# A new rule for how many expert slots each pair of steps gets, and casts moved from VectorE to ScalarE

## The chip, the cores and the metric

The kernel runs on one core of a Trainium2 chip. The core has a matrix engine (TensorE, PE in the profile; its weight loads are the rows PEld), a vector engine (VectorE, DVE), an activation engine (ScalarE, ACT), a general engine that here issues indirect transfers (GpSimd, POOL), a queue engine for plain transfers (SyncE, SP), and 16 DMA engines that all queues share. The metric is the device time of one execution in microseconds (us); lower is better.

## The reference

The input is 2048 tokens of 512 numbers. They are normalised once (layer norm), and two branches are added to the input:

- **Attention** with 32 heads of 16 and one shared key and value head: `softmax(q k^T / 4) v`, then a projection with `wo`.
- **Experts.** For each token, 32 heads of two queries of 128 are scored against 64 keys each (`s1`, `s2`). The kernel contracts the query projection with the keys, so that a score costs one product with a combined weight. The best two of `s1` and of `s2` give four candidate sums; the best two of these name two of the 4096 experts and, by a softmax, two gates. An expert has a vector u and a vector v: the output adds `gate * gelu(x . u) * v` over 32 heads x 2 experts.

```python
top_e = jnp.take_along_axis(eidx, ord2, axis=-1)
g = _softmax(top_s, axis=-1)
ue = u[top_e]
ve = v[top_e]
act = _gelu(jnp.einsum("nd,nhkd->nhk", xf, ue))
out = jnp.einsum("nhk,nhk,nhkd->nd", g, act, ve)
```

## The kernel before

**Staging.** The 2048 tokens are four groups of 512 (phases 0 to 3). A prologue, whose order a scheduler decides, normalises and transposes all tokens, makes q, k, v and the weights and scores of the first eighth of the heads. All the rest is one loop over d, of 256 pairs of attention steps and 24 turns more (from line 1104), in an order written out by hand: each engine gets its instructions in the order in which the Python emits them. Below, a turn of this loop is called a step, and the first is 0.

**Attention in a step.** `att_steps` issues four pieces of scores on PE (L317), whose exps run on ACT (L320, four per step), and the products with the values (L331). After every eight steps ACT copies the sums out of PSUM into tile `e` (L339). Two of these copies make a block that is divided by its sums: a tile `rsb` is loaded, and DVE multiplies (`on`, L380). `e` and `rsb` take turns on one buffer.

**Experts, phases 0 and 1: gathered.** A *slot* is one candidate for a tile of 128 tokens: an indirect DMA of POOL's queue fetches 128 rows of u and v (`g`, 512 KB, L842), DVE forms the dot products with x (L854), and adds gate times v to the sum later (L889). Four slots share a chain of small DVE instructions (L863 to L865), a tanh on ACT (L870) and the weight `w` (L877). There are 512 slots. A ring of 12 buffers holds gathered rows; a slot's buffer comes free with its add, and only then can the gather 12 slots further on be issued. `lent` takes two buffers of the ring for the weights `wo` during parts of the loop. In each step `mid` runs the dots, then the adds that are ready, then up to four gathers.

**Experts, phases 2 and 3: dense.** Here all 4096 experts are multiplied with 512 tokens. A one-hot stage builds the table of gates: DVE makes one-hot tiles (L713 to L716), PE multiplies them (L729), ACT copies the result, and it goes through memory (`dg`). Then 32 blocks of 128 experts follow: PE multiplies x with u (`pact`, L781), DVE and ACT form the gated gelu (L800 to L808), PE multiplies with v (`pout`, L764), DVE adds to the sum (L767). ACT rounds the weights of a block and DVE makes the rest (L677, L678).

**Scores.** `item` (L531) makes the scores of 128 tokens and four heads: 12 matmuls, then 8 maxima and 8 index searches on DVE (L541, L543); after four items `batch` works out the indices and gates. In the first pass over the heads (phase 0), `wp_make` first builds the combined weights of four heads: PE multiplies (L486), ACT copies, PE transposes (`pwt`, L493), and DVE rounds the result to the matmul's format (L495) and subtracts that from the exact value (L496), so that `wk` holds a high and a low part.

**What sets the order.** `score_thread` is a Python generator with a planned cost for each piece of PE's expert work; `fill` draws pieces from it in each step until a plan that rises evenly over the loop is met. How many slots a step gets is counted by `pos`: up to step 191 it rises by fixed amounts that depend on whether the step has scores, one-hot work or blocks (`dense_on` 0, 2 or 1), and from step 192 on by an even share of what is left. Both PE's pieces and the slots' own order stay the same whatever `pos` does; `pos` decides beside which of PE's pieces a slot's dot and add stand in DVE's queue. The one-hot stages are steps 64 to 87 and 182 to 201; the blocks follow them, to steps 134 and 252.

PSUM has three buffers under the tag "x", which the score, transposition, weight, one-hot and block products take in turn.

Of the kernel before, what the change touches and what calls it, by code (L numbers as in the profile page):

```python
# [31 lines left out]
KC = D // P  # L32
NC = 8
TPH = GT
NPH = NGRP
NSP = 2
NB = 32
# [10 lines left out]
C_CUB = 0.044715 * C_IN  # L48
MOST = 4.8
UNIT = 0.235  # L50


@with_exitstack
def tile_kernel(ctx, tc, x, wq, wkv, wo, wqT, kT, uv, ub, vb, out):
    nc = tc.nc
# [409 lines left out]
    def wp_load(c, h):  # L465
        if late[0] is None or (c == 1 and h < 2):
            w = gtile(F32, (P, 2, D), "wqt") if c == 0 and h > 1 else big.tile([P, 2, D], F32, name="wqt", tag="wqt", bufs=2)
        else:
            w = late[0].tile([P, 2, D], F32, name="wqt", tag="gy", bufs=3)
        nc.sync.dma_start(w, wqT[4 * c + h].rearrange("(s p) d -> p s d", p=P))  # L470
        WC["raw", c, h] = w

    def wk_tile():
        return big.tile([P, 2, 512], F32R, name="wk", tag="wk", bufs=NWK)

    def wp_make(c):

        wt = [big.tile([P, 2, 512], F32, name="wt", tag="da", bufs=2) for _ in range(2)]
        for h in range(4):
            for n in range(4 * c + h + 1, min(4 * c + h + 3, 4 * NC) if late[0] else 4):  # L480
                if ("raw", n // 4, n % 4) not in WC:
                    wp_load(n // 4, n % 4)
            w = WC.pop(("raw", c, h))
            p = xtile("pw")
            for s in range(2):
                nc.tensor.matmul(p[s * E:(s + 1) * E, :], kTs[:, s, :], w[:, s, :], start=True, stop=True)  # L486
            nc.scalar.copy(wt[h // 2][:, h % 2, :], p)
            yield 0.9
        WC[c] = []
        for k in range(KC):  # L490
            p = xtile("pwt")
            for h in range(4):
                nc.tensor.transpose(p[:, h * P:(h + 1) * P], wt[h // 2][:, h % 2, k * P:(k + 1) * P], ident)  # L493
            wk = wk_tile()
            nc.vector.tensor_copy(wk[:, 0, :], p)  # L495
            nc.vector.tensor_tensor(out=wk[:, 1, :], in0=p, in1=wk[:, 0, :], op=OP.subtract)  # L496
            WC[c].append(wk)
            store(lambda k=k, wk=wk: nc.sync.dma_start(d_w[c][:, k], raw(wk[:])))
            yield 0.45

    def wp_read(n, ks=range(KC)):
        for k in ks:
            wk = wk_tile()
            nc.sync.dma_start(raw(wk[:]), d_w[SEQ[n][1]][:, k])
            WC.setdefault(n, []).append(wk)
# [6 lines left out]
    def item(n_, ti):  # L512
        ph, c = SEQ[n_]
        nph, nc_ = SEQ[n_ + 1] if n_ + 1 < len(SEQ) else (None, None)
        t = TPH * ph + ti
        g, j = divmod(t, GT)
        b, jb = divmod(ti, BT)
        if jb == 0:
            m8 = small.tile([P, BT, 8, 8], F32, name="m8", bufs=1)
            i8 = small.tile([P, BT, 8, 8], U32, name="i8", bufs=1)  # L520
            M8[ph, c, b], I8[ph, c, b] = m8, i8
        m8, i8 = M8[ph, c, b], I8[ph, c, b]
        p = xtile("psc")

        last = ti == TPH - 1
        more = nc_ is not None and not (ph >= NSP and c == NC - 1)
        read = more and n_ + 1 >= NC
        n = 0
        for k in range(KC):
            for a, bb in TERMS:  # L530
                nc.tensor.matmul(p, XT[g][k][:, a, j * P:(j + 1) * P], WC[n_][k][:, bb, :],  # L531
                                 start=n == 0, stop=n == 11)
                n += 1
            if read and ti == 0 and k < 2:
                wp_read(n_ + 1, range(2 * k, 2 * k + 2))
            if last and more and nph != ph:
                load_phase2_xt(nph, k)
            if k < KC - 1:
                yield 3 * UNIT
        for s in range(8):  # L540
            nc.vector.max(m8[:, jb, s, :], p[:, s * E:(s + 1) * E])  # L541
        for s in range(8):
            nc.vector.max_index(i8[:, jb, s, :], m8[:, jb, s, :], p[:, s * E:(s + 1) * E])  # L543
        if jb == BT - 1:
            batch(ph, c, b)
        yield 3 * UNIT

    IDX, G = {}, {}
# [95 lines left out]
    def dense(DG, after):  # L644
# [15 lines left out]
        def fetch_gates(b):  # L660
            if b < NB:
                if formed[0] < b - 2:
                    flush()
                gy = late[0].tile([P, 2, 512], F32, name="gy", tag="gy", bufs=3)
                nc.sync.dma_start(gy[:, 0, :], d_g[b])
                gates[b] = gy
# [31 lines left out]
        for n, src in enumerate((df1, df2, dgt)):  # L698
            if n == 2:
                yield None  # L700
            p = xtile("ptd")
# [7 lines left out]
        def onehot(q):  # L709
            if q < NQ:  # L710
                tb = q * TB
                oa = kt(F16, (P, P, TB))
                nc.vector.tensor_tensor(out=oa, in0=io, in1=bc(0, tb, P), op=OP.is_equal)  # L713
                ob = kt(F16, (P, NB, TB))
                nc.vector.tensor_tensor(out=ob, in0=io[:, :NB, :], in1=bc(1, tb, NB), op=OP.is_equal)
                nc.vector.tensor_mul(ob, ob, bc(2, tb, NB))  # L716
                OH[q] = oa, ob

        onehot(0)
        onehot(1)  # L720
        for q in range(NQ):
# [5 lines left out]
            p = xtile("pg")  # L727
# [26 lines left out]
        def sums():  # L754
# [4 lines left out]
            for j in range(GT):  # L759
# [7 lines left out]
                nc.vector.tensor_add(acc, acc, p)  # L767
                yield 6 * UNIT

# [3 lines left out]
        for b in range(NB):  # L773
            if b not in splits:
                flush()
            us, vs = splits.pop(b)
            p = xtile("pact")
            n = 0
            for k in range(KC):
                for a, c in TERMS:  # L780
                    nc.tensor.matmul(p, us[:, a, k * P:(k + 1) * P], XT[DG][k][:, c, :],  # L781
                                     start=n == 0, stop=n == 11)
                    n += 1
                if k == 0:
                    store(lambda b=b: fetch_gates(b + 1))
                    if b % 2 == 0:
                        later_split(b + 2)
                if k == KC - 1 and b == NB - 1 and after is not None:
                    wp_read(after, range(2))
                if b == NB - 1 and after is not None:  # L790
                    load_phase2_xt(SEQ[after][0], k)
                if k < KC - 1:
                    yield 3 * UNIT
            wd = late[0].tile([P, 2, 512], F32R, name="wd", tag="wd", bufs=4)
            if b not in gates:
                run(STORES)
            gy = gates.pop(b)
            g, y = gy[:, 0, :], gy[:, 1, :]

            nc.scalar.activation(y, p, AF.Square, scale=C_CUB ** 0.5)  # L800
            stt(y, y, C_IN, p, op0=OP.add, op1=OP.mult)
            stt(g, g, 1.0 / GS, p, op0=OP.mult, op1=OP.mult)
            LAST.append(lambda y=y: nc.scalar.activation(y, y, AF.Tanh))
            behind(lambda y=y, g=g, wd=wd: stt(wd[:, 0, :], y, 1.0, g, op0=OP.add, op1=OP.mult))
            behind(lambda y=y, g=g: stt(y, y, 1.0, g, op0=OP.add, op1=OP.mult))

            def rest(y=y, wd=wd):
                nc.vector.tensor_tensor(out=wd[:, 1, :], in0=y, in1=wd[:, 0, :], op=OP.subtract)  # L808
                formed[0] += 1

            behind(rest)
            held.append((wd, vs))
            yield 3 * UNIT
            if b % 2:
                later_split(b + 2)
                if ready:
                    yield from sums()
                else:
                    yield None
                ready, held = held, []  # L820
# [10 lines left out]
    NSL = len(slots)  # L831
# [62 lines left out]
    g_next, d_next, a_next, a_ready = [0], [0], [0], [0]  # L894
# [41 lines left out]
    def flush():  # L936
        posts()
        run(LAST)
        run(LATER)
        run(ON_ACT)  # L940
        run(BEHIND)
# [8 lines left out]
    def load_phase2_xt(g, k):  # L950
        if k == 0:
            XT[g] = []
        xt = big.tile([P, 2, 512], F32R, name="xt", tag="xt", bufs=4)
        nc.sync.dma_start(raw(xt[:]), d_xt[g - 1][k])
        XT[g].append(xt)
# [11 lines left out]
                yield from dense(ph, n + 1 if n + 1 < len(SEQ) else None)  # L967
                dense_on[0] = 0

    dense_on = [0]  # L970
    sgen = score_thread()
    spent = [0.0]

# [126 lines left out]
    with tc.manual_schedule(engines={E_.PE, E_.Activation, E_.DVE, E_.Pool, E_.SP}):  # L1100
        done0 = spent[0]
        half = STEPS // 2
        pos = 0.0
        for d in range(half + 24):


            if d < half * 3 // 4:
                pos += 2.4 if len(IDX) < NC * TPH else (1.9, 2.3, 1.5)[dense_on[0]]
            else:
                pos += max(0.0, NSL - pos) / max(half - 4 - d, 1)  # L1110

            todo = min(int(pos + 0.001), NSL) - d_next[0]

            def mid():
                post = POST[:]
# [97 lines left out]
```

## Time and profile before

| | us |
|---|---|
| median of three runs | 2036.56 |
| range of these runs | 2034.71 to 2038.64 |
| the profiled execution | 2035.25 |
| its span, first to last instruction | 2033.5 |

The profile has one execution. It gives each engine's busy time, groups of instructions with the idle time ahead of them and what ended it ("<-" names the releaser), and the timeline. L12 is line 12 of the kernel, and tile names stand as out<-in. Busy times of matmuls are modelled, and an instruction's time overlaps its neighbours' a little, so that for short instructions the spacing in the timeline is the better price. The mean granted clock of TensorE was 0.959. The loop's first exp starts at 148.6 us, the last ends at 2012.1.

### The profile page before, as it was taken

What the parts mean: (1) busy time and instruction counts of PE and PEld (TensorE: products, weight loads), DVE (VectorE), ACT (ScalarE), POOL (GpSimd) and SP (SyncE); (2) the same over time, 40 slices, a digit from 0 to 9 for tenths busy, and PEclk for the clock granted to TensorE, in tenths of its full rate; (3) what the DMA queues carried; (4) which work ended last, traced back from release to release, by engine and by line L of the source; (5) the groups of instructions that cost most, each with busy time, mean ns of one, the idle gap of its engine ahead of it and who ended that gap; (6) DMA issues with size and microseconds to landing.
All of it is one profiled execution on the core that took longest, in us unless ns stands there. A gap on an engine that the chain in (4) does not pass through costs nothing.

```text
span 2033.5 us, 34691 instructions
## 1 busy us (share of the span) xinstructions
PE 1889.3 (93%) x10990; PEld 1006.7 (50%) x10990; DVE 1742.0 (86%) x6809; ACT 1245.1 (61%) x1710; POOL 585.9 (29%) x542
## 2 busy tenths in 40 slices
PE   6869989999988998899999999999979989999997
PEld 4634444455544453555555545554545435555553
DVE  7638898989998876889989779999999778999993
ACT  3236555555546787577767565555558747777773
POOL 2202233322222232334424332222223233333310
PEclk9989999999998898999999999999989889999998
DMA  7856788886764778677888878777558887778751
GB/s 273 303 190 216 274 286 292 315 312 231 259 222 116 214 226 263 215 245 237 264 269 279 309 264 284 285 239 239 184 175 233 264 272 242 251 236 264 234 193 63
DMA packets 239882, 494.79 MB, mean 243 GB/s; under 512 B 93380, under 2 KB 93380, under 8 KB 239692
## 3 DMA queue, kind: packets, MB, share of 16 engines
q0 software_dynamic: 73728, 268.47, 39.8%
q1 hardware_dynamic: 163960, 222.44, 33.4%
q10 hardware_dynamic: 2004, 1.61, 0.3%
q8 instruction: 88, 1.44, 0.3%
q14 instruction: 102, 0.84, 0.1%
HBM read 429.51 MB, written 57.64 MB: 240 GB/s over the span
## 4 chain that ended last, share of the span: by engine, by line
PE 56%; DVE 26%; DMA 5%; issue 3%; ACT 3%; SPq 1%; another core or an unknown queue 0%; ACTq 0%; DVEq 0%
PE pv L331 16%; PE sc L317 11%; PE psc L531 10%; PE pact L781 7%; PE pout L764 6%; DVE xa L889 5%; DVE i L543 4%; DVE g L854 4%; DVE m L541 3%; PE pwo L426 2%; PE pg L729 2%; ACT pt L320 2%; DMA gy<-dg 1%; DVE oh L713 1%; DVE wk L678 1%
## 5 line engine op out<-in xcount | busy, mean ns | idle before, releaser
L320 ACT ACTIVATE pt<-sc 128x1024 f32<-128x1024 f32 x1024 | 993.3, 1025 | 558.3 <-PE sc L317 520.1
L842 POOL DMA_INDIRECT g<-in_uv_dram,idx x512 | 569.1, 1111 | 1374.8 <-DVE xa L889 753.3
L331 PE MATMUL pv<-pt,vaug 128*32 128x512 f32 x4096 | 517.4, 624 | 0.0
L317 PE MATMUL sc<-qa,kaug 64*128 64x512 f32 x2048 | 394.0, 459 | 27.8 <-ACT pt L320 26.7
L531 PE MATMUL psc<-wk,xt 128*128 128x512 f32 x1536 | 384.8, 401 | 15.8 <-DVE wk L496 6.7
L889 DVE SCALAR_TENSOR_TENSOR xa<-g,w,xa 128x512 f32<-128x512 f32 x512 | 371.3, 749 | 0.0
L854 DVE CUSTOM_DVE_ANT_0 g<-g,xa 128x512 f32<-128x512 f32 x512 | 338.6, 686 | 0.0
L531 PEld LDWEIGHTS psc<-wk,xt 128*128 128x128 f32 x1536 | 282.3, 189 | 110.1 <-issue 32.4
L317 PEld LDWEIGHTS sc<-qa,kaug 64*128 64x128 f32 x2048 | 159.5, 189 | 352.4 <-ACT pt L320 222.2
L331 PEld LDWEIGHTS pv<-pt,vaug 128*32 128x32 f32 x4096 | 110.0, 112 | 261.9 <-issue 260.2
L764 PE MATMUL pout<-wk,wd 128*128 128x512 f32 x768 | 198.2, 406 | 10.6 <-DVE da L767 4.4
L543 DVE FIND_INDEX8 i<-m,psc 128x8 uint32<-128x64 f32 x1024 | 207.4, 229 | 0.0
L781 PE MATMUL pact<-xt,wk 128*128 128x512 f32 x768 | 197.1, 403 | 4.3 <-DVE da L767 4.3
L764 PEld LDWEIGHTS pout<-wk,wd 128*128 128x128 f32 x768 | 142.4, 190 | 58.8 <-DVE da L767 6.8
L781 PEld LDWEIGHTS pact<-xt,wk 128*128 128x128 f32 x768 | 140.8, 189 | 53.7 <-issue 17.9
L541 DVE MAX8 m<-psc 128x8 f32<-128x64 f32 x1024 | 146.7, 219 | 17.6 <-PE psc L531 15.3
L877 DVE SCALAR_TENSOR_TENSOR w<-gth,ga 128x4 f32<-128x4 f32 x128 | 20.7, 162 | 95.5 <-ACT gth L870 93.2
L767 DVE TENSOR_TENSOR da<-da,pout 128x512 f32<-128x512 f32 x128 | 82.9, 684 | 8.8 <-PE pout L764 8.7
L678 DVE TENSOR_TENSOR wk<-rw,wk 128x512 fp32r<-128x512 f32 x128 | 84.6, 688 | 3.9 <-ACT wk L677 3.9
L729 PE MATMUL pg<-oh 128*128 128x32 f16 x1024 | 73.7, 246 | 10.0 <-DVE oh L716 9.2
L713 DVE TENSOR_TENSOR oh<-oh 128x2048 f16<-128x2048 f16 x64 | 78.0, 1220 | 5.6 <-PE pg L729 5.6
L729 PEld LDWEIGHTS <-oh 128*128 128x128 f16 x1024 | 68.6, 164 | 21.8 <-issue 10.1
(151 smaller groups left out, 1373.8 us busy)
## 6 DMA issues: line engine op xcount, KB each, us to landing
wk<-dw SPq DMA_DIRECT2D x96, 512.0 KB
wqt<-in_wqT_dram SPq DMA_DIRECT2D x32, 512.0 KB
dw<-wk SPq DMA_DIRECT2D x32, 512.0 KB
rw<-in_ub_dram SPq DMA_DIRECT2D x64, 256.0 KB
rw<-in_vb_dram SPq DMA_DIRECT2D x64, 256.0 KB
dg<-gst SPq DMA_DIRECT2D x32, 512.0 KB
gy<-dg SPq DMA_DIRECT2D x64, 256.0 KB
qa<-dqh SPq DMA_DIRECT2D x128, 64.0 KB
```

The lines of the kernel that those rows point to most:

```text
L317: nc.tensor.matmul(p[:, b, :], kaug[o:o + 64, kc * P:(kc + 1) * P], QA[u][o:o + 64, i, :], start=True, stop=True)
L320: nc.scalar.activation(pt, p, AF.Exp, scale=SCALE)
L331: nc.tensor.matmul(PV[u][32 * j:32 * j + 32, :], vaug[:, kc, :], pt[:, b, :], start=kc == 0, stop=kc == 15)
L531: nc.tensor.matmul(p, XT[g][k][:, a, j * P:(j + 1) * P], WC[n_][k][:, bb, :], start=n == 0, stop=n == 11)
L541: nc.vector.max(m8[:, jb, s, :], p[:, s * E:(s + 1) * E])
L543: nc.vector.max_index(i8[:, jb, s, :], m8[:, jb, s, :], p[:, s * E:(s + 1) * E])
L729: nc.tensor.matmul(p[:, i * NB:(i + 1) * NB], oa[:, :, i], ob[:, :, i], start=True, stop=True)
L764: nc.tensor.matmul(p, wd[:, a, j * P:(j + 1) * P], vs[:, c, :], start=n == 0, stop=n == 5)
L781: nc.tensor.matmul(p, us[:, a, k * P:(k + 1) * P], XT[DG][k][:, c, :], start=n == 0, stop=n == 11)
L842: nc.gpsimd.indirect_dma_start(out=gt, out_offset=None, in_=uv, in_offset=bass.IndirectOffsetOnAxis(ap=IDX[ph, c, ti][:, s:s + 1], axis=0))
L854: nc.vector.tensor_tensor_reduce(u, u, XN[TPH * ph + ti], scale=1.0, scalar=0.0, op0=OP.mult, op1=OP.add, accum_out=a[:, i:i + 1])
L889: nc.vector.scalar_tensor_tensor(acc, v, w[:, i:i + 1], acc, op0=OP.mult, op1=OP.add)
```

## The change

Two things change.

First, the count of slots. A new counter `vec` adds up estimated times of VectorE's other work as it is emitted: scores of an item, a batch, the subtraction of a transposed weight, a pair of one-hot tiles, a block. From the total of these and of 512 slots at 1.35 the kernel works out a mean per step, which is taken at 0.82 in steps of the one-hot stages. In each step the allowance rises by the mean, and the slots follow from what `vec` leaves of it, at most four more per step, and never more than have been gathered. All slots are due by step 252.

Second, in `wp_make` the rounding copy of a transposed weight out of PSUM is issued on ACT instead of DVE; the subtraction stays on DVE.

```diff
+V_ITEM, V_BATCH, V_SUB, V_OH, V_BLOCK, V_SLOT = 2.64, 3.0, 0.7, 1.97, 5.45, 1.35
+OH_PART = 0.82
...
             wk = wk_tile()
-            nc.vector.tensor_copy(wk[:, 0, :], p)
+            nc.scalar.copy(wk[:, 0, :], p)
             nc.vector.tensor_tensor(out=wk[:, 1, :], in0=p, in1=wk[:, 0, :], op=OP.subtract)
+            vec[0] += V_SUB
...
+        vec[0] += V_ITEM
         if jb == BT - 1:
             batch(ph, c, b)
+            vec[0] += V_BATCH
...
                 OH[q] = oa, ob
+                vec[0] += V_OH
...
             held.append((wd, vs))
+            vec[0] += V_BLOCK
...
-    dense_on = [0]
+    dense_on, vec = [0], [0.0]
...
         pos = 0.0
+
+        others = (NPH * NC * (TPH * V_ITEM + V_BATCH) + NC * KC * V_SUB
+                  + (NPH - NSP) * (512 // 16 * V_OH + NB * V_BLOCK))
+        mean = (others - vec[0] + NSL * V_SLOT) / (half - 4 - (1 - OH_PART) * 24 * (NPH - NSP))
+        room = vec[0]
         for d in range(half + 24):
-            if d < half * 3 // 4:
-                pos += 2.4 if len(IDX) < NC * TPH else (1.9, 2.3, 1.5)[dense_on[0]]
-            else:
-                pos += max(0.0, NSL - pos) / max(half - 4 - d, 1)
-            todo = min(int(pos + 0.001), NSL) - d_next[0]
+            room += mean * (OH_PART if dense_on[0] == 2 else 1)
+            pos = max(pos, min(pos + 4.0, (room - vec[0]) / V_SLOT, NSL) if d < half - 4 else NSL)
+            todo = min(int(pos + 0.001), NSL, g_next[0]) - d_next[0]
```

## The prediction

> **What bounds the kernel now.** I read the page first, then busy times by stage, then the waits, then the timeline at every idle gap of PE.
>
> ```profile
> span 2033.5 us, 34691 instructions
> ...
> PE 1889.3 (93%) x10990; PEld 1006.7 (50%) x10990; DVE 1742.0 (86%) x6809; ACT 1245.1 (61%) x1710; POOL 585.9 (29%) x542
> ...
> q0 software_dynamic: 73728, 268.47, 39.8%
> ```
>
> PE is full on average and VectorE (DVE) nearly so: what a stage is worth depends on which of the two is ahead there. I call one turn of the loop over d a step. It issues four exps (L320), so every fourth exp in the timeline begins one. Undisturbed steps last 3.40 us plus 0.966 us per unit of the planner's cost (6.81 us at 3.525, 7.49 at 4.23, 8.17 at 4.935). Steps of the one-hot stages last 5.35 us at 4.0.
>
> In the busy times below the stretches are steps 1-31, 32-63, 88-134, 135-147, 148-181 and 182-201; columns are length, then PE, PEld, DVE, ACT, POOL, the granted clock and DMA.
>
> ```profile
> 152.40:394.60 242.20, 224.74 (x1274) 111.03 (x1274) 215.47 (x1083) 136.59 (x177) 74.12 (x72) 0.97 0.79 272
> 394.60:630.70 236.10, 222.59 (x1250) 121.08 (x1248) 225.56 (x1470) 128.38 (x158) 61.42 (x60) 0.98 0.73 249
> ...
> 789.70:1147.00 357.30, 341.58 (x1883) 188.61 (x1881) 326.41 (x726) 248.64 (x343) 131.06 (x106) 0.98 0.78 255
> 1147.00:1238.60 91.60, 90.27 (x487) 44.60 (x485) 70.49 (x402) 54.12 (x68) 27.23 (x27) 1.00 0.76 261
> 1238.60:1482.60 244.00, 238.19 (x1343) 130.85 (x1341) 235.85 (x1534) 136.55 (x167) 63.16 (x63) 0.99 0.73 250
> 1482.60:1619.90 137.30, 122.26 (x1032) 63.83 (x1030) 125.15 (x324) 101.31 (x166) 43.68 (x35) 0.89 0.78 219
> ```
>
> DVE is idle only in 135-147 (21 us of 92), and in the first one-hot stage, 64-87 (119 us busy of 159). By the undisturbed steps, the excess is 30 us in 1-31, 18 in 32-63, 22 in 64-87, 27 in 88-134, 2 in 135-147, 9 in 148-181, 28 in 182-201 and 19 in 202-252: 155 us in all.
>
> The timeline shows how DVE's delay becomes PE's. At step 168:
>
> ```profile
> 1387.15 0.68 DVE L380 TENSOR_TENSOR on<-ot,rsb 128x512 f32<-128x512 f32 x1
> 1387.91 0.59 ACT L339 COPY e<-pv 128x512 f32<-128x512 f32 x1 [7.05 <-issue]
> 1389.67 1.71 PE L317 MATMUL sc<-qa,kaug 64*128 64x512 f32 x4 [4.03 <-ACT pt L320]
> ```
>
> Tile e has one buffer, shared with rsb, so ACT's copy waits for DVE's "on" once in 16 steps (d = 8 mod 16). DVE ended its work of step 167 8.9 us after the first exp of 168 (I call this behind), and PE lost 4.9 us and 2.1 in the next step at a lower clock. Step 56 is the same (10.9 us behind, 6.6 + 2.7 lost). While weights are transposed, PE waits for the casts directly, at step 24:
>
> ```profile
> 335.90 0.69 DVE L495 CAST wk<-pwt 128x512 fp32r<-128x512 f32 x1
> 336.62 0.69 DVE L496 TENSOR_TENSOR wk<-pwt,wk 128x512 fp32r<-128x512 f32 x1
> ...
> 337.46 0.77 PE L531 MATMUL psc<-wk,xt 128*128 128x512 f32 x1 [3.71 <-DVE wk L496]
> ```
>
> **The change part by part.** On DVE a slot costs 0.61 us for the dot, 0.66 for the add (their spacing in the timeline) and 0.10 as its quarter of four small ones: 1.37 us. Counting dots by the old and the new rule (before/after): 74/73 in steps 1-31, 61/51 in 32-63, 36/49 in 64-87, 108/97 in 88-134, 25/41 in 135-147, 65/57 in 148-181, 36/28 in 182-201, 105/112 in 202-252. The other engines' work per step stays, except for the casts.
>
> *Casts.* 32 of DVE's 0.69 us (spacing 0.61) go to ACT, where the same shape out of PSUM takes 0.59 (L178). 28 are inside the loop, four in each of seven steps or pairs of steps (5, 9/10, 14/15, 19, 23/24, 28, 32). In those steps ACT comes to 6.7 to 7.9 us against PE's 6.5 to 7.5: up to 1 us late, made good in the next step (4.1 us). DVE's chain to PE falls from two to one operation per k: at step 24 psc starts 1.3 us sooner, and the 3.71 us gap drops to 2.4, so that the 2.7 us lost to half clock behind it go too. Step by step I take -4 (24), -3.5 (10), -1.8 (15), -1.5 (19), -1 each for 5, 28 and 16, -0.5 (14), and +2 for ACT: **-12** (ends -18, all of the 27 us of excess in these steps but a third; -3, step 24 alone with ACT late). In the prologue ACT gains four casts (2.4 us) and loses two table loads (1.28 us each, L580 and L150), which the new order makes needless: **-1** (-2.6 to +2.4).
>
> *Slots out of 32-63.* 9.4 us less for DVE, which no longer drops 11 us behind: the losses at 53, 56 and 57 go, 1.6 + 6.6 + 2.7: **-11** (-13 to -7). Next is PE's own 6.81.
>
> *One-hot, 64-87.* No dots at 66-70: the 6.2 us of excess in 66-72 fall to 1.7 (ACT's 5.7 us per step is next), -4.5. But the slots return in fours at 73-87: DVE has 61 us of work in 73-83, where the steps took 65, and gathers issued one step ahead make it wait some 4 us: +2. Four dots ahead of the one-hots at 65: +1; 85-87: +1.5. Sum **0** (-6 to +6).
>
> *Block loop, 88-134.* At 90, 95 and 120 PE waited 3.11, 4.29 and 4.12 us for DVE's gy (L802) and da (L767) behind a crowded queue. The new rule takes 2 to 3 us of slots out of the queue of each: -4.5, -4, -3.5. Steps 115 and 118 get four dots and four adds; their 9.1 to 9.4 us of DVE work is about the most that passed before without loss (9.1 at 109): +1. **-11** (-17 to -3).
>
> *135-147.* Here the rule runs out of gathers. It wants four slots a step; the ring of 12 is cut to 10 by the loan (lent) to 143, 10 slots are dotted and not yet added, and every dot from 135 to 147 takes a gather that was issued in the step before, behind an add. Before, it was two to six steps. POOL issues them like this:
>
> ```profile
> 1194.01 0.93 POOL L842 DMA_INDIRECT g<-in_uv_dram,idx  x1 [4.68 <-DVE den L603]
> 1195.25 1.20 POOL L842 DMA_INDIRECT g<-in_uv_dram,idx  x1 [0.31 <-issue]
> 1196.76 0.94 POOL L842 DMA_INDIRECT g<-in_uv_dram,idx  x1 [0.30 <-DVE m L541]
> ```
>
> By q0's packets (128 of 4 KB each) a gather lands 5.4 us after issue (median; quickest 3.7). The third of a burst lands 9.5 us after the first's issue (median of 110), 7.7 in the quiet rows above. I take the middle, 8.6. The loop on DVE is: first add, third landing (8.6), third dot and weight (0.8), first add (0.7): 10.1 us per step. DVE's other work fits beside it. Thirteen turns are 131 us, and 2 more for the steps of four. Queued behind the waiting dot are the weight, the adds, the max and index of the scores; ACT's tanh waits for its chain, and ACT's exps behind that: PE can be about 3.5 us behind the add, no more. So 134-147 lasts 133 us where it lasted 98: **+35** (+10 if a third gather lands in 2.5 + 4.2 us; +46 at 9.5).
>
> *148-181.* DVE enters about 10 us behind, PE waits 1 us twice, and ACT's copy of e at 152 meets it as at 56: +2, +7.5, +2.7: **+12** (0 to 14). From there 8.7 us fewer of slots: step 168 loses nothing (-7), and at 182, where PE needs the whole of DVE's work (8.15 us gap), the delay is 6 instead of 11: -6. **-13** (-16 to -5).
>
> *182-201.* 184-189 have two dots instead of nine: 36 us become 32. 190-199, which DVE filled, -4.5; less clock loss at 183: -1.5. **-10** (-15 to -3).
>
> *202-252.* At 202 the gates wait 11.1 us on their DMA (L802), which SP issues behind the stores of dg: stays. 207 -1; the dots of 209 wait on gathers of 208, +3; +1 more: **+3** (0 to 10).
>
> Sum: -12 - 1 - 11 + 0 - 11 + 35 + 12 - 13 - 10 + 3 = -8. The profiled execution took 2035.25 us (span and 1.75), 1.3 under the median of 2036.56: **2027 us**.
>
> [...]
>
> **The rivals.** *The ring decides (slower).* The third gather lands at 9.5 us or later: DMA already runs at 0.76 there and gathers rise by half. +46 instead of +35, the fours at 73-87 and 209 cost 5 more each, and a quarter of the -58 is taken up by other waits (+14): 2027 + 11 + 10 + 14 = 2062; between that and the point lies 2050, which I give it. It decides from 10.7 us per turn, with all else as summed. Against it: a stretched step moves less other data per us.
>
> *The loop is short (much faster).* Bursts land as in the quiet rows (7.7: +23) or as 2.5 + 3.9 of the quick single ones (6.4: +6): 2015 to 1998, say 2007. [...]
>
> *No net change.* DVE's leads are lost to waits that its load does not set, like the DMA at 202, and the two sides cancel: 2036.
>
> **How the numbers follow.** 0.2% (4 us) is about what a measurement can tell. The point's case 0.42 (own range 2016 to 2040; faster 0.28, same 0.10, slower 0.04), short loop 0.18 (faster), ring 0.28 (slower), no net change 0.12 (0.04, 0.03, 0.05). Faster 0.50, same 0.13, slower 0.37. The range runs from 2000, short of the quickest loop, to 2058, short of the dearest ring.
>
> **What would show it.** Casts: gap of PE ahead of psc at step 24 under 2.5 us. 56: no wait of ACT's e. 135-147: DVE idle ahead of the dots on the gather's DMA, a line that is absent now, and about 133 us for 134-147. 152: a wait of e of 7 us or more. 168: none. The prediction is wrong if the dots of 135-147 do not wait, or if they also wait elsewhere for over 10 us.

## The result and the profile after

The changed kernel takes 2066.4 us (median of 4 runs, 2064.9 to 2069.3), the kernel before 2036.0 beside it: the ratio is 1.0149, interval 1.0132 to 1.0167. It is 30 us slower where 2027 was forecast. Its profiled execution took 2066.42 us.

The page of the changed kernel, its first lines and the group of the dots (after the bar: busy us and mean ns; then idle time before them and what ended most of it):

```profile
span 2064.7 us, 34720 instructions
...
PE 1906.6 (92%) x10990; PEld 1008.5 (49%) x10990; DVE 1726.0 (84%) x6777; ACT 1259.6 (61%) x1740; POOL 589.5 (29%) x542
...
L862 DVE CUSTOM_DVE_ANT_0 g<-g,xa 128x512 f32<-128x512 f32 x512 | 334.0, 684 | 65.4 <-DMA g<-in_uv_dram,idx 61.7
```

DVE is busy 16 us less than before (1742.0), and the span is 31 us longer: the added time is waiting. The dots' 61.7 us on their gathers is a line that the kernel before has not got. The waits of the changed kernel (us in total, times, longest) show who else waits:

```profile
DVE g L862 <- DMA g<-in_uv_dram,idx: 61.7, 35, 6.6
...
PE sc L320 <- ACT pt L323: 47.3, 40, 8.6
...
ACT gth L878 <- DVE gy L872: 42.4, 8, 8.0
```

In steps 134-147 they are one chain: a dot waits for its gather, ACT's tanh (gth) for the dot's sums, ACT's next exps stand behind the tanh in ACT's queue, and PE's scores wait for the exps. 44.1 of the 61.7 us lie there, 42.0 of the 42.4 and 17.8 of the 47.3 (PE's longest, 8.6, is at step 88). In the kernel before, PE's wait for the exps was 26.7 us in all, and none of it lay there.

Where the time came from is read by stage. Busy times of the changed kernel over steps 1-31, 32-63, 64-87, 88-134, 135-147, 148-181 and 182-201 (columns as in the prediction: length, PE, PEld, DVE, ACT, POOL, granted clock, DMA):

```profile
153.20:385.00 231.80, 222.20 (x1271) 109.38 (x1271) 198.99 (x1049) 148.91 (x200) 72.17 (x71) 0.98 0.80 280
385.00:612.90 227.90, 221.18 (x1250) 120.83 (x1248) 217.71 (x1455) 128.16 (x158) 54.65 (x54) 0.99 0.74 246
612.90:777.40 164.50, 152.09 (x1155) 73.93 (x1155) 133.66 (x300) 118.64 (x186) 53.04 (x45) 0.88 0.75 224
777.40:1132.50 355.10, 338.53 (x1883) 186.19 (x1881) 313.70 (x683) 248.37 (x341) 119.39 (x96) 0.98 0.73 244
1132.50:1266.90 134.40, 104.24 (x487) 47.96 (x485) 87.76 (x451) 54.56 (x71) 43.23 (x42) 0.88 0.73 245
1266.90:1509.90 243.00, 237.89 (x1343) 130.57 (x1341) 233.74 (x1526) 136.13 (x166) 60.81 (x60) 0.99 0.72 240
1509.90:1647.20 137.30, 126.01 (x1032) 64.48 (x1030) 112.02 (x289) 101.20 (x163) 29.64 (x27) 0.86 0.67 182
```

Against the lengths before (242.2, 236.1, 159.0, 357.3, 91.6, 244.0, 137.3) that is -10.4, -8.2, +5.5, -2.2, +42.8, -1.0 and 0.0; the prologue gives +1.1 and 202-252 +4.8. One stage costs more than the whole loss. In 135-147 neither PE (104 of 134) nor DVE (88 of 134) is full. The last row is as telling: DVE has 13 us less to do than before (112.02 against 125.15), and the stage lasts as long.

The timeline of the changed kernel at the start of the slow stage:

```profile
1141.36 0.69 DVE L862 CUSTOM_DVE_ANT_0 g<-g,xa 128x512 f32<-128x512 f32 x1 [1.97 <-DMA g<-in_uv_dram,idx]
...
1143.92 0.69 DVE L862 CUSTOM_DVE_ANT_0 g<-g,xa 128x512 f32<-128x512 f32 x1 [1.86 <-DMA g<-in_uv_dram,idx]
...
1144.61 0.74 DVE L897 SCALAR_TENSOR_TENSOR xa<-g,w,xa 128x512 f32<-128x512 f32 x1
...
1145.63 1.28 POOL L850 DMA_INDIRECT g<-in_uv_dram,idx  x1 [11.63 <-DVE gq L871]
...
1152.83 2.08 PE L429 MATMUL pwo<-wo,on 128*128 128x512 f32 x2 [6.86 <-DVE on L383]
1152.86 0.59 ACT L342 COPY e<-pv 128x512 f32<-128x512 f32 x1 [10.33 <-issue]
```

The reader sees one turn of the loop that the prediction described: the second and third dot wait for their gathers, then comes the first add, which frees a buffer, and only then does POOL issue the next gather, after 11.6 us of standing still (the bracket names gq, the small instruction right behind that add). DVE's "on" of step 136 stands behind all that and behind 16 maxima and indices of scores, so PE and ACT's copy of e wait for it too.

### The profile page after: what moved, and what is told of

The parts are those of the page before. It is cut to its first block, busy times and chain, and to the rows that moved or that the text cites. A ratio compares the mean times of both kernels' runs of the same rounds, so it can differ in the third digit from the quotient of the medians.

```text
span 2064.7 us, 34720 instructions
## 1 busy us (share of the span) xinstructions
PE 1906.6 (92%) x10990; PEld 1008.5 (49%) x10990; DVE 1726.0 (84%) x6777; ACT 1259.6 (61%) x1740; POOL 589.5 (29%) x542
## 4 chain that ended last, share of the span: by engine, by line
PE 60%; DVE 17%; DMA 9%; issue 4%; ACT 3%; SPq 1%; POOL 0%; ACTq 0%; DVEq 0%; POOLq 0%
PE pv L334 18%; PE sc L320 12%; PE psc L535 12%; PE pact L788 6%; PE pout L771 6%; DVE xa L897 4%; DMA g<-in_uv_dram,idx 4%; PE pg L736 3%; DVE g L862 3%; DVE i L547 3%; DVE m L545 2%; ACT pt L323 2%; DMA out_dram<-fin 1%; DMA fin<-dpart 1%; PE pwo L429 1%
## 5 line engine op out<-in xcount | busy, mean ns | idle before, releaser
L334 PE MATMUL pv<-pt,vaug 128*32 128x512 f32 x4096 | 532.5, 640 | 0.0
L320 PE MATMUL sc<-qa,kaug 64*128 64x512 f32 x2048 | 397.4, 461 | 48.8 <-ACT pt L323 47.3
L862 DVE CUSTOM_DVE_ANT_0 g<-g,xa 128x512 f32<-128x512 f32 x512 | 334.0, 684 | 65.4 <-DMA g<-in_uv_dram,idx 61.7
L736 PE MATMUL pg<-oh 128*128 128x32 f16 x1024 | 74.0, 247 | 11.6 <-DVE oh L722 10.8
L547 DVE MATCH_VALUE_LOAD i<-m,psc 128x8 f32 x1024 | 74.1, 72 | 0.0
```

The lines of the kernel that those rows point to most:

```text
L320: nc.tensor.matmul(p[:, b, :], kaug[o:o + 64, kc * P:(kc + 1) * P], QA[u][o:o + 64, i, :], start=True, stop=True)
L334: nc.tensor.matmul(PV[u][32 * j:32 * j + 32, :], vaug[:, kc, :], pt[:, b, :], start=kc == 0, stop=kc == 15)
L736: nc.tensor.matmul(p[:, i * NB:(i + 1) * NB], oa[:, :, i], ob[:, :, i], start=True, stop=True)
L862: nc.vector.tensor_tensor_reduce(u, u, XN[TPH * ph + ti], scale=1.0, scalar=0.0, op0=OP.mult, op1=OP.add, accum_out=a[:, i:i + 1])
```

## The experiments

The runs came in three groups, each on one chip beside the kernel before: the casts, the slots, the reserve and the first try with the one-hots (before 2041.4 us there); the loop, the fewer slots, the second try and the slots by stage (2038.6); the last three (2039.6).

**The casts alone.** The kernel before, with one line changed.

```diff
-            nc.vector.tensor_copy(wk[:, 0, :], p)
+            nc.scalar.copy(wk[:, 0, :], p)
```

> The kernel before with only the cast of the transposed weights moved to ACT. Theory (the terms of the sum are separate): steps 1-31 take 10 us less than before, nothing else changes by more than 3 us, and the time is 2026 (2020 to 2030). Rival (the casts' gain came from the changed slots, which leave DVE freer there): steps 1-31 gain less than 4 us, time 2032 to 2037.

2021.5 us, ratio 0.9896 (0.987 to 0.9921). Steps 1-31 lasted 232.0 us, 10.2 less than before, and the same in the changed kernel (231.8). So the casts' term is shown, and it does not need the new rule for the slots. The rest did not stay within the 3 us that was expected: with unchanged slots, 88-134 took 353.0 us (4.3 less) and 182-201 took 142.4 (5.1 more). The whole is 20 us under before on that chip, twice what these steps gave.

**The slots alone.** The changed kernel with the cast back on DVE (the diff above reversed).

> The changed kernel with the cast left on DVE: the slot rule alone. Theory: steps 1-31 as in the kernel before, 134-147 at about 140 us where before has 98, the whole 2076 (2070 to 2082), 40 us over before. Rival (ACT's added casts shift the later work and part of the loss is theirs): under 2062.

2069.5 us, ratio 1.0122 (1.0098 to 1.0147), just under the low end of what was expected, and 28 over before on that chip where 40 was expected. Its profile bears the stages out: 241.2 us in 1-31, as before, and 143.2 in 134-147 where the kernel before has 97.7 and the changed one 140.5. Nothing here puts a part of the loss down to ACT's added casts. But the whole times do not simply add up: the casts alone won 20 us, while the changed kernel, which has them, is 30 over before, and this one, which has not, 28 (each on its own chip).

**Three gathered slots kept in reserve.** The changed kernel may dot only what leaves three gathered slots undotted:

```diff
-            todo = min(int(pos + 0.001), NSL, g_next[0]) - d_next[0]
+            todo = min(int(pos + 0.001), NSL, g_next[0] - (3 if g_next[0] < NSL else 0)) - d_next[0]
```

> The changed kernel, with three gathered slots always kept undotted, so that a dot takes a gather that was issued at least two steps before. It does 29 dots in 135-147 where the changed kernel does 41 and the kernel before 25, and 72 in 148-181 instead of 57. Theory (the loop through the gather sets 135-147): the waits of the dots on the gathers' DMA fall from 62 to under 15 us, 134-147 takes 105 us instead of 140, 148-181 some 5 us more than the 243, and the whole is 2036 (2028 to 2045). Rival (DVE's load of slots sets these steps, and the wait is only where it shows): 12 slots fewer at 1.37 us give 16 us, moved to 148-181: 134-147 at 122 or more, the whole 2055 or more.

2034.1 us, ratio 0.9955 (0.9928 to 0.9983). Busy times in steps 134-147 of this run:

```profile
1130.20:1226.20 96.00, 96.00 (x523) 47.87 (x521) 75.13 (x414) 58.14 (x73) 28.86 (x29) 1.00 0.84 277
```

The dots' line in its waits:

```profile
DVE g L862 <- DMA g<-in_uv_dram,idx: 5.6, 5, 2.3
```

PE is busy in all of the 96 us at full clock, and the dots' waits are gone. Against the changed kernel, 45 us of this stage are gone. Two things differ: how far ahead each gather is issued, and 12 dots that moved on to 148-181. At 1.37 us each these dots are 16 us at most, so most of the 45 is the distance; and with all its dots the changed kernel's DVE was busy in only 93.5 us of its 140.5. Some 15 came back in 148-181 (258.0 us, with 72 dots where the changed kernel has 57), three times what was expected. DVE is busy in 252 of the 258 us there, so that its load probably sets the time; no run tested that. The reserve does not make the rule a gain: on the same chip the casts alone took 2021.5 us, 12.5 less than this kernel, which has both.

**The loop put into the kernel before.** Three slots a step in 134-147, paid back in 148-181:

```diff
+            pos += 2.1 if d == 134 else 1.1 if 134 < d < 148 else -0.48 if 148 <= d < 182 else 0.0
-            todo = min(int(pos + 0.001), NSL) - d_next[0]
+            todo = min(int(pos + 0.001), NSL, g_next[0]) - d_next[0]
```

> The kernel before with three slots a step instead of 1.9 in 134-147 (39 dots in 135-147 instead of 25), paid back by 16 fewer in 148-181, so that in 135-147 each dot takes a gather of the step before, as in the changed kernel; casts and all else as before. Theory (that loop by itself is the loss): 134-147 lasts 135 to 143 us where before has 98, 148-181 loses 5 to 10, and the whole is 25 to 37 over before. Rival (the loss needs the changed kernel's lag and lumps from the steps ahead): 134-147 under 120, the whole under 15 over before.

2064.0 us, ratio 1.0121 (1.0061 to 1.018): 25 over before. Busy times in its steps 134-147:

```profile
1143.50:1271.70 128.20, 107.28 (x523) 50.72 (x521) 88.86 (x456) 58.15 (x74) 40.41 (x39) 0.91 0.73 249
```

The dots' line in its waits:

```profile
DVE g L854 <- DMA g<-in_uv_dram,idx: 34.2, 18, 5.6
```

128 us is less than the 135 expected, though over the rival's 120. From step 144 on the ring has 12 buffers again, and here one or two gathered slots are left over in 145-147; the changed kernel takes four in 145 and 146 and leaves none there. 148-181, with 16 slots fewer, was to lose 5 to 10 us and lost 3.2 (240.8). DVE stands idle in 39 of the 128 us, so it is not the added dots that fill the stage. The loop alone, in an otherwise unchanged kernel, costs most of what the whole change lost: 25 us of 30.

**Fewer slots where the gates are loaded.** The changed kernel with its lumps of four taken out of 84-100:

```diff
-            pos = max(pos, min(pos + 4.0, (room - vec[0]) / V_SLOT, NSL) if d < half - 4 else NSL)
+            pos = max(pos, min(pos + (1.0 if 84 <= d <= 88 else 2.5 if 88 < d <= 100 else 4.0),
+                               (room - vec[0]) / V_SLOT, NSL) if d < half - 4 else NSL)
```

> The changed kernel with at most 1 slot in each of steps 84-88 and 2.5 in 89-100 where it has up to 4; the ring's steps 134-147 are as in the changed kernel. Theory (twelve gathers in 85-87 fill the DMA queues just ahead of the gates' load, so DVE's L809 waits 4.4 us on it with four dots ahead and PE stands 8.6 us at 88): step 88 falls from 13.35 to about 8 us and 80-91 by 5 to 8 us, and the whole stays some 24 us over before (19 to 28). Rival (the gates' load is late whatever the gathers do, as at 202): step 88 stays over 12 us and the whole 28 to 34 over before.

2062.6 us, 24 over before (ratio 1.0117, 1.0056 to 1.0178); the interval is wide. Step 88 fell from 13.35 to 9.42 us, and 88-90 together from 34.2 to 31.7. Steps 80-87 fell from 58.0 to 51.2, but nearly all of that lies in 80-83 (32.2 to 25.5), where the slots are those of the changed kernel: that was not the edit. The lumps do cost at 88: with them the step takes 13.35 us here, 13.8 in the run with the slots alone and 19.3 in the one with the reserve; in the ten profiles without them it takes 6.4 to 9.4. The timeline of the changed kernel at the gates' load, from its issue on SP to DVE's first use of it:

```profile
768.62 3.73 SPq L671 DMA_DIRECT2D gy<-dg  x3
...
776.23 0.69 DVE L862 CUSTOM_DVE_ANT_0 g<-g,xa 128x512 f32<-128x512 f32 x1 [1.89 <-DMA g<-in_uv_dram,idx]
...
782.32 0.69 DVE L809 SCALAR_TENSOR_TENSOR gy<-gy,pact 128x512 f32<-128x512 f32 x1 [4.44 <-DMA gy<-dg]
782.92 2.73 DVE L897 SCALAR_TENSOR_TENSOR xa<-g,w,xa 128x512 f32<-128x512 f32 x4
...
785.57 0.68 DVE L383 TENSOR_TENSOR on<-ot,rsb 128x512 f32<-128x512 f32 x1
786.34 0.59 ACT L342 COPY e<-pv 128x512 f32<-128x512 f32 x1 [6.97 <-issue]
```

DVE's instruction in the timeline of this run:

```profile
773.95 0.69 DVE L809 SCALAR_TENSOR_TENSOR gy<-gy,pact 128x512 f32<-128x512 f32 x1 [4.30 <-DMA gy<-dg]
```

DVE waits as long with 4 gathers in 85-87 as with 12 (4.30 and 4.44 us), but only because it comes to the wait earlier. From SP's first issue to DVE's use the load takes 13.7 us in the changed kernel (768.62 to 782.32) and 8.8 in this run (765.19 to 773.95); in the kernel before it is 8.1. The 16 DMA engines are full in the first and the third stretch (a share of 1.03 and of 1.04), and q0, the queue of the gathers, moves 3.19 MB in the first, 1.08 in the second and 1.05 in the third, beside 2.2 to 2.3 MB of q1, which has the loads. So the theory's reason is borne out: the twelve gathers share the engines with the gates' load and make it some 5 us later. The rest of what the edit took away stands around that wait on DVE: dots that wait for gathers ahead of it, and four adds behind it, ahead of "on", for which ACT's copy of e waits.

**The one-hot matmuls in two places.** In 182-201 less load on DVE had gained nothing, and in the clock's records of both profiles the grant goes between 1.00 and 0.50 on a grid of 3.41 us. Of the eight windows from 1578.5 to 1605.8 us of the kernel before four are at 0.50, and three of the six from 1604.3 to 1624.8 of the changed kernel, where PE has no gap over 0.3 us. The first try, on the kernel before (`part` runs the score thread for one group of 16 one-hot matmuls):

```diff
             pv(pu, pk)
+            if oh_on[0]:
+                part()
             pv(pu, pk + 1)
```

> The kernel before; in the one-hot stages (65-84 and 184-200) one of the two groups of 16 one-hot matmuls of a step is moved from the step's end to between the two pv groups. No dot is moved. In both profiles PE's clock is granted by windows of 3.41 us, and a window is at half clock when in the one ahead PE streamed under about 2.05 us, if a one-hot matmul (32 columns, spaced at 0.07 us) is counted at 0.023 us; 32 of them in a row bring a window to that with no gap in PE. Theory (the clock, not DVE, held the one-hot steps): the half-clock windows of steps 67-71, 83, 188 and 196-198 go, ten windows of some 1.7 us lost each; DVE is next at once, with 125 us of work in the 137 of 182-201, so about half of it is gained: 2027 (2020 to 2032). Rival (DVE fills these steps and the clock costs nothing): 2034 to 2038.

2052.8 us, ratio 1.0066 (1.0035 to 1.0097): slower, and neither theory had that. The low windows of steps 67-71, 83, 188 and 196-198 did go, and the mean clock of 182-201 rose from 0.89 to 0.94. But the steps lasted 6.2 us; ACT's copies of the first group, which now stood ahead of its exps, were the first suspect.

**The same with ACT's copies left at the step's end.**

```diff
-                post = POST[:]
-                POST.clear()
+                post = [] if split[0] else POST[:]
+                if not split[0]:
+                    POST.clear()
```

> As the earlier run that puts one of a step's two groups of one-hot matmuls between the pv groups, but with ACT's copies of that group's results left until the step's end, where the kernel before has them (there they stood ahead of the exps, and every step lasted 6.19 us). Theory (the half-clock windows follow from too little streaming in the window ahead, and they hold the one-hot steps): no half-clock window in 66-79 and 186-199 without a gap of PE ahead, and 182-201 lasts 131 us (127 to 135) where before has 137 and the earlier run 143; the whole 5 to 12 under before. Rival (DVE holds these steps): the clock is full and 182-201 still lasts 136 or more.

2047.4 us, ratio 1.0049 (1.0023 to 1.0076). Steps 184-199 of this run:

```profile
1517.90:1619.00 101.10, 92.67 (x850) 47.89 (x848) 96.33 (x204) 80.35 (x138) 41.12 (x28) 0.99 0.82 233
```

The clock is full there (0.99), as the theory said, and the stage is 143.0 us, as the rival said. In 66-80 four stretches at half clock stayed, each behind a gap of PE of 0.6 to 0.9 us. Most steps last 6.2 us again, whether one dot stands in them or two, so it was not the copies. PE's own rows are part of that: the two groups of 16 take 1.25 us each and the two halves of pv 1.07, where the kernel before has 2.23 for 32 one-hots together and 1.92 for 16 pv, 0.5 us in all. The rest was not settled. The clock can be freed in this way (0.99 against 0.90 in these steps), but the way costs more than the clock did (182-201 lasts 143.0 us against 137.3); with DVE busy in 96 of these 101 us, it may be what comes next.

**Hardly any slots in the one-hot steps.** The question that the last two left open, on the kernel before: 4 slots in 184-199, the others later.

```diff
+            if 184 <= d < 200:
+                pos = last + (1 if 190 <= d < 194 else 0)
+            last = pos
```

> The kernel before with 4 slots instead of 26 or so in steps 184-199; they are done in 202-252. Only the steps 184-199 are read. Theory (the clock holds these one-hot steps, DVE is behind it by little): with 30 us less on DVE they still last 91 to 98 us where before has 97.7, with four half-clock windows or more and no gap of PE ahead of them. Rival (DVE fills them, as the prediction had it): they fall to PE's 5.35 a step, 88 us or less.

Steps 184-199 of this run (one execution):

```profile
1512.60:1610.80 98.20, 95.96 (x850) 49.41 (x848) 65.56 (x112) 79.75 (x129) 8.78 (x6) 0.88 0.55 134
```

Of the kernel before:

```profile
1507.80:1605.50 97.70, 94.45 (x850) 49.17 (x848) 95.23 (x203) 80.31 (x135) 34.41 (x27) 0.90 0.86 233
```

And of the changed kernel:

```profile
1533.20:1631.50 98.30, 96.38 (x854) 49.57 (x856) 82.19 (x165) 80.12 (x132) 17.95 (x16) 0.88 0.69 179
```

DVE's work goes from 95 to 82 to 66 us, and the length stays at 98. DVE was busy there; in these three runs it was not what the steps waited for. What the runs show beside that length is the clock. Busy times in six neighbouring windows of the run with hardly any slots:

```profile
1522.20:1525.60 3.40, 3.40 (x44) 2.68 (x40) 2.51 (x5) 3.14 (x7) 1.15 (x1) 1.00 0.96 252
1525.60:1529.00 3.40, 3.40 (x20) 0.59 (x16) 2.47 (x5) 2.48 (x4) 0.00 (x0) 0.50 1.16 319
1529.00:1532.40 3.40, 3.40 (x42) 2.70 (x40) 1.21 (x2) 2.48 (x4) 0.00 (x0) 1.00 0.61 161
1532.40:1535.80 3.40, 3.40 (x20) 0.65 (x18) 2.67 (x6) 2.48 (x4) 0.00 (x0) 0.51 0.89 190
1535.80:1539.30 3.50, 3.50 (x46) 2.56 (x38) 1.05 (x1) 2.41 (x4) 0.00 (x0) 0.99 0.67 139
1539.30:1542.70 3.40, 3.40 (x16) 0.99 (x20) 2.84 (x6) 2.55 (x5) 0.00 (x0) 0.50 0.01 2
```

PE's timeline over the first two of them:

```profile
1522.94 2.23 PE L729 MATMUL pg<-oh 128*128 128x32 f16 x32
1525.10 0.82 PE L317 MATMUL sc<-qa,kaug 64*128 64x512 f32 x4
1525.86 3.47 PE L331 MATMUL pv<-pt,vaug 128*32 128x512 f32 x16
```

PE is busy in every one of them, and every second one has half the clock: the one behind a window with 32 one-hot matmuls. The 16 pv then take 3.47 us instead of 1.92.

**Slots by stage, by hand.** The casts, and an even rate in each stage in place of the rule:

```diff
-            if d < half * 3 // 4:
...
+            rates = ((32, 2.36), (64, 1.63), (88, 1.65), (135, 2.4), (148, 2.2), (182, 1.7), (202, 1.4))
+            pos += next((r for e, r in rates if d < e), max(0.0, NSL - pos) / max(half - 4 - d, 1))
```

> The kernel before with the casts on ACT and an even rate of slots in each stage, fitted by hand to DVE's other work: 52 dots in 32-63 (before 61), 40 in 64-87 (36), 113 in 88-134 (108), 28 in 135-147 (25), 58 in 148-181 (65), 28 in 182-201 (36), 118 in 202-252 (105). No step has over 3 slots and at least three gathered slots stay undotted. Theory (the idea of the rule is right, its lumps and the ring's loop lose it): 10 us from the casts, 7 in 32-63, 6 in 148-181, 3 in 182-201, given back 4 in the stages with more slots: 22 us under before (16 to 28), and under the kernel with the casts alone by 7 or more. Rival (the slots' places earn nothing): 8 to 12 under before.

2022.7 us, ratio 0.9918 (0.9894 to 0.9942): 16 under before, the edge of what was expected. That it beats the casts alone by 7 is not shown: these were 20 under before, on another chip. By stages it gained in 32-63 (226.9 us), 148-181 (240.0), 182-201 (134.8) and 202-252 (366.4), and lost in 64-87 (167.5) and 88-134 (360.6), where it has more slots than before. In 64-87 the slots need not be the reason: 49.0 us were at half clock there, before 36.4.

**The same without the losses, beside the casts alone.**

```diff
-            if d < half * 3 // 4:
-                pos += 2.4 if len(IDX) < NC * TPH else (1.9, 2.3, 1.5)[dense_on[0]]
+            if d < 202:
+                pos += (1.63 if 32 <= d < 64 else 2.2 if 135 <= d < 148 else 1.75 if 148 <= d < 182 else 1.3 if d >= 182
+                        else 2.4 if len(IDX) < NC * TPH else (1.9, 2.3, 1.5)[dense_on[0]])
```

> The kernel before with the casts on ACT and its own rates of slots, but 1.63 in 32-63 (52 dots instead of 61), 2.2 in 135-147 (28 instead of 25), 1.75 in 148-181 (60 instead of 65), 1.3 in 182-201 (26 instead of 36) and the rest in 202-252 (125 instead of 105): where more slots cost time in the run with an even rate by stage (1-31, 64-87, 88-134), the rates of before stay. Theory (what that run gained and lost by stage adds up): 10 from the casts, 7 in 32-63, 4 in 148-181, 3 in 182-201, up to 6 in 202-252: 24 to 30 us under before, and 12 to 18 under the casts alone. Rival (the stages do not add, since a shift of the stages moves the clock's half windows by as much): 5 or less under the casts alone.

> The casts alone once more, beside the run above on the same chip. Theory: 10 to 18 us under before, 232 us for steps 1-31 again; 182-201 anywhere from 131 to 143 with the same instructions, since the half-clock windows fall otherwise in every run.

2013.6 us with the mended rates, ratio 0.9886 (0.986 to 0.9912), and 2026.4 with the casts alone, 0.9942 (0.9923 to 0.996). The mended rates are 26 us under before and 13 under the casts: faster than both kernels of this case. Not every stage came as summed. 32-63 lasted 236.6 us in its profile, since PE stood 4.5 us on a load of xt in step 39 and 3.3 us of the stall at 56 returned. Against the profile of the casts alone, 148-181 gave 4.8 us, 182-201 gave 4.2, and 202-252, which was to give up to 6, gave 1.2. These two profiles are 19 us apart, and 11 of these lie in 64-87 and 88-134, where the rates are the same. So the 13 us are measured, but how much of them the slots' places earn is not shown. The casts alone gave 232.8 us in 1-31 again, and 140.3 in 182-201.

## Why the prediction failed, step by step

The forecast was 2027 us, faster, within 2000 to 2058; 2066 came, slower and beyond that range. The step that failed worst is 182-201 with step 182: 16 us were counted there, most of them because DVE was read as setting the time; the stage did not change, and what the runs show in DVE's place is the clock. The ring's term was too small by 8, 88-134 by 9 and 64-87 by 5.5.

*Where it went right.* The casts: -10.4 where -12 stood. The gap ahead of psc at step 24, under 2.5 us by the forecast, is 1.88. 32-63: -8.2 where -11 stood (-13 to -7). 202-252: +4.8 where +3 stood. And the mechanism of 135-147: the dots wait on gathers of the step before, the line that was absent is there, and with a reserve the 45 us go.

*Its other signs.* It called itself wrong if the dots also wait elsewhere for over 10 us, and they do: 17.6 of the 61.7 us lie in steps 75-87 and 201-204. At 152 the wait of e is 4.7 us, where 7 or more stood. At 56 the copy of e still waits 3.9, but on PE's own scores; at 168 PE no longer waits.

*The ring's size.* The term was +35, from 10.1 us a turn; it measured +42.8, within its ends. From the first add of step 134 (1129.2 us) to that of 147 (1268.8) are 13 turns of 10.7 us: 0.6 more in each, 8 us in all. By q0's packets the third gather landed 7.7 to 9.3 us after the first's issue in most turns, as taken, but 12.9 and 12.1 us after it in the bursts of 134 and 144. The rival "the ring decides" had 0.28, and its 2062 us is nearest to what came, in part by luck. A turn of 10.7 us was its threshold: with all else as summed, that gives the time of before, 2036. The ring was dearer, as it said, but its own +46 did not come, and the other 31 us were lost in other stages.

*182-201, the step that failed in kind.* "190-199, which DVE filled, -4.5", and -4 for 184-189: nothing came, and -10 became 0. DVE's row of 125 in 137 us was read as DVE setting the time. The run with hardly any slots there shows it did not. By steps 182-201 of the eleven profiles whose one-hot matmuls stand as before (half-clock time is what the clock's records add up to in the stretch):

| run | dots | us | at half clock, us |
|---|---|---|---|
| loop in the kernel before | 36 | 131.3 | 23.9 |
| before | 36 | 137.3 | 30.7 |
| casts alone, again | 36 | 140.3 | 37.5 |
| casts alone | 36 | 142.4 | 47.8 |
| reserve | 26 | 129.9 | 27.3 |
| slots alone | 28 | 133.4 | 30.7 |
| changed | 28 | 137.3 | 37.5 |
| fewer slots at the gates | 28 | 136.2 | 34.1 |
| slots by stage | 28 | 134.8 | 30.7 |
| mended rates | 26 | 136.1 | 37.5 |
| hardly any slots | 12 | 139.9 | 41.0 |

At equal half-clock time 8 to 10 dots fewer are worth 2.5 to 4 us (137.3 against 134.8 and 133.4; 140.3 against 137.3 and 136.1), and with 12 dots nothing more is gained. With the slots unchanged the stage goes from 131.3 to 142.4 us as its half-clock time goes from 23.9 to 47.8.

*88-134: -11 forecast, -2.2 measured.* The three stalls were costed by what the new rule takes out of the queue ahead of them. 120 gave more than that (-5.9 for -3.5), though by luck in part: in six other profiles with the old slots step 120 lasts 8.2 to 10.3 us, where the profile of before has 13.0 and the changed kernel 7.1. 90 and 95 gave less (-2.7 for -4.5, -1.4 for -4). In 95 PE still stands 3.7 us on DVE's da with no dot in the step. And step 88, of which the prediction said nothing in this stage, cost 5.3, and 89 another 1.0: the lumps of four at 85-87 fell on the gates' load. They were counted at +1.5 for 85-87, as DVE work, and not as gathers that fill the DMA engines beside a load that DVE waits for.

*64-87: 0 forecast, +5.5.* 66-72 gave -2.2 of the -4.5; 66 to 68 ran at a clock of 0.69 to 0.80. 73-83, costed at +2, lost 8.1, all of it in 80-83. The gathers, as costed, make dots wait there, the last two 2.6 and 1.3 us at 80. But with the same slots and like waits (2.1 and 1.5) the run with fewer slots from 84 on was 6.7 us shorter in 80-83; it had 3.4 us at half clock there, the changed kernel 10.9. If PE sets the time there, 7.5 us more at half clock cost 3.7: by this estimate about half of the loss is the clock, and why it fell in one execution and not in the other is not settled.

*148-181 and 182.* +12 and -7 were forecast for 148-181, and -1.0 came. The wait at 152 was to cost 7.5 us and more, +12 with its neighbours; step 152 took 2.3 us more, 148-153 together 4.3. The new rule has no dots at 148 and 151, which probably lets DVE catch up; that was in the counts and was not used. 168 and 169 gave 6.1 of the 7. Step 182, -6 by the forecast, gave 2.4.

By steps, the point and the profiled execution (2066.4) differ by 39 us: 8 in 135-147, 16 in 182-201 (-10 and the -6 of 182, against 0), 9 in 88-134, 5.5 in 64-87, -6 in 148-181 and 8 for the small ones (32-63, the casts, the prologue, 202-252), which makes 40.

## What to carry to other kernels

A rule that hands out work by an engine's free time needs a second limit: how old a prefetched buffer must be before it is used. Look at the distance in steps between issue and use, and at what frees the buffer; here, with a distance of one, the transfer's latency was in the loop, though DVE was idle in 47 of the stage's 134 us. Look also at what else the DMA engines carry when a lump of gathers is issued: here a load that DVE waits for took 13.7 us, and 8.1 without the lump. And a full engine in a stage's row is not yet its bound (95, 82 and 66 us of DVE's work in the same 98 us): compare the same stage in executions with more and less of that work, and look at the granted clock, before counting a lighter load as time.

## What the hardware showed beyond that

In the clock's records of the kernel before and of the changed kernel the grant goes between 1.00 and 0.50 on a grid of 3.41 us. A one-hot matmul (32 columns, one every 0.07 us with its own weights) is counted here at 0.023 us of streaming and all others at their busy time. Then all 25 full-clock windows in the loop of the kernel before that precede a half-clock one had streamed 2.05 us or less, and of the 480 that precede a full one only 6 had. In the changed kernel it is 32 of 32, and 13 of 475. The 0.023 us is an estimate fitted to these two profiles, and the 2.05 us move with it. In four others (casts alone, the loop, the mended rates, hardly any slots) the same count holds for 107 of 108 half-clock windows, and 44 of 1886 full ones follow such a window too.

In these profiles gaps of PE of 1.88 us (step 24 of the changed kernel) and 1.90 (step 15 of the kernel before) are followed by a half-clock window. So are windows with no gap of PE, filled with short matmuls: in the run with hardly any slots PE is busy throughout the six windows above, and three of them have 0.50 or 0.51.

It would fit these records that the time of such a stage depends on where it falls on that grid, but no run shows it. The kernel with the casts alone has the same instructions in both of its runs; its profiled spans differ by 12 us (2018.7 and 2030.7), 7 of them in 64-87 (157.6 us with 27 at half clock, 164.7 with 39).
